# Q and K of the first two token tiles from padded weight rows on 32-column tiles of TensorE, with a reordered front of an adaLN, local-attention and MLP block

## The chip, the cores and the metric

The kernel runs on one core of a Trainium2 chip. The core has five engines that run side by side, each with its own queue of instructions: TensorE (PE; loads of its weights are listed as PEld), VectorE (DVE), ScalarE (ACT), GpSimd (POOL) and SyncE (SP), which here issues DMA transfers and DMA transposes. The metric is the device time of one execution in microseconds (us), and a kernel's time is the median of its runs.

## The reference, cut to what matters

One block over 2048 tokens of 448 features: an attention with a sliding dilated window (8 positions, 2 apart, 16 heads of 28 features), then an MLP with 1792 hidden features, both modulated by a condition c.

```python
mod = silu(c) @ w_mod                      # 448 -> 6 x 448
sa, ca, ga, sb, cb, gb = mod
h = layernorm(x) * (1 + ca) + sa
q, k, v = h @ wqkv                         # 16 heads of 28
attn = softmax(q . k[pos - 2*(0..7)] / sqrt(28))   # 8 keys for a token
x = x + ga * ((attn . v) @ wo)
h = layernorm(x) * (1 + cb) + sb
x = x + gb * (gelu(h @ w1 + b1) @ w2 + b2)
```

All inputs are bf16.

## The kernel before

**Tiles.** Tokens are held as eight tiles of 128 partitions; a partition holds two neighbouring tokens (even and odd), so the window of step 2 becomes 8 neighbouring columns of one parity. A contraction over 448 features is made of three steps of 128 rows and one of 64. The tail of 64 features is written twice into a tile, so that 64-row products can use either half of the rows.

**The front of a tile.** The rows of x are loaded (SP, L339, into x_all). DVE takes the statistics of each token (BN_STATS L456, BN_AGGR L458, into stt and mvs). The reciprocal deviation rs_all comes from ACT (Ln and Exp, L466 and L467) or POOL (a power, L469). DVE normalises into a buffer zy (L478), and the tail is copied (DVE L488 or L491, POOL L490). Tiles 0 and 1 are transposed by TensorE (L535, against ident, into PSUM ptr); tiles 2 to 7 by a DMA transpose (SP, L527, into zT). DVE (L502) or ACT (L504) then applies the modulation and writes hT, features by tokens.

**The modulation.** c is spread over partitions by TensorE into PSUM ps_c. silu(c) is made by ACT's exp (e_c, L392), DVE's add and reciprocal (L394, L395) and product (L396, silu_bf), and ACT widens it to 32 columns (L398, silu_bc). Products with w_mod give the columns of sa and ca (mod_col, L425, "column constants" below). The other four rows of the modulation come later from products on 32-column tiles of TensorE (L641).

**Q and K.** Attention needs Q and K with features on partitions, every head on 32 partitions. For tiles 0 and 1, `front_qk` takes the weights as the fixed side, four heads of 28 columns at a time. `spread` (L432 to L450) first copies the weight rows wqk_st and wqr_st into Wqk and Wqr, in which each head has 32 columns; these are ten copies on DVE, ACT and POOL. One product then covers four heads (128 columns) over 256 token columns: L562 in the first group, which goes row step by row step as the copies come, and L548 after it, with the 64-row step in L554. ACT (L609) copies each result to qT or kT. Tiles 2 to 7 (`natural_qk`) take hT as the fixed side and the weight rows as they are (L548 with wqk_st), and a DMA transpose puts the result into qT or kT. After tile 1 come the first scores (L738, PSUM lt) and the first value product (L706, PSUM pv).

**Order.** Nothing is scheduled at run time. Every step is recorded as a task with a number, its engine, what it reads and writes, and the buffers that it uses. `ORDER` lists the numbers in the sequence in which the tasks are written into the engines' queues; `n:A`, `n:D` or `n:P` puts a task on ACT, DVE or POOL, and `n+k@m` puts k dummy products on warm_w (L382) ahead of it, to fill TensorE's waits. `SLOTS` gives each buffer its place. Each queue runs in order. The loads go through SP in one sequence, and SP waits for an earlier transfer of the same one of eight lanes before it issues the next.

**Batches.** Attention runs in nine batches of 114 columns of each parity, with the tiles of the next batch prepared beside it; an output projection and the MLP of two tiles at a time follow as their batches are done.

## Time and profile before

| what | value |
|---|---|
| three runs | 168.0, 168.93, 170.48 us (median 168.93) |
| the profiled execution | 169.75 us, of which the span is 168.1 us |
| TensorE clock granted | 1.00 |
| TensorE busy | 161.5 us (96%) |
| DVE, ACT, POOL busy | 115.8 us (69%), 102.7 us (61%), 47.7 us (28%) |
| instructions | 4962 |
| DMA | 18.78 MB |

The span is what the profiler's instructions cover; 1.65 us of the profiled execution lie around it. Start times in the views count from the start of the span. A row of an engine's timeline gives the start in us, the length in us, the engine, the line, the operation with its result and operands, the tile or shapes, and how many instructions of that kind the row joins; in square brackets stands a wait ahead of it, with what ended it. Where a row joins several products of TensorE that run one behind the other, it ends a little later than the next row begins, since products overlap. In the view by stretches each engine is given by its busy time and, in brackets, the number of its instructions, in the order PE, PEld, DVE, ACT, POOL; then come the granted clock, the busy share of the DMA engines and GB/s. In the groups by line the columns are busy us and mean ns of one, then idle us ahead of it.

### The profile page before, as it was taken

The page shows a single profiled execution, that of the slowest core. Times are in us where ns is not written, and L with a number is a line of the kernel's source. Part 1 is how long each engine was busy: PE and PEld are TensorE (multiplying, and loading weights), DVE is VectorE, ACT ScalarE, POOL GpSimd, SP SyncE. Part 2 cuts the span into 40 slices and gives each one's busy share as a digit, 9 for nine tenths or more (in the row PEclk, how much of TensorE's full clock was granted, in tenths as well). Part 3 has the DMA queues.
Part 4 walks back from the last instruction along what each step waited for, and adds up shares of the span by engine and source line. Part 5 has one row for each costly group of instructions (what it writes and reads, how often), then busy time and mean ns, then how long its engine had stood idle before and what let it go on. Part 6 is the DMA issues. An engine that isn't in the chain of part 4 may idle for free.

```text
span 168.1 us, 4962 instructions
## 1 busy us (share of the span) xinstructions
PE 161.5 (96%) x2126; PEld 83.4 (50%) x2126; DVE 115.8 (69%) x271; ACT 102.7 (61%) x142; POOL 47.7 (28%) x76
## 2 busy tenths in 40 slices
PE   7989989999997999999999999999999999999992
PEld 4768544345544544435565444556434455444562
DVE  6869899879899689998738877474798930400032
ACT  3368987779489954759866376956627730097300
POOL 4135252300361201269300113820003870007200
PEclk9999999999999999999999999999999999999999
DMA  5999989799997999910091000008110027110003
GB/s 153 325 335 297 168 265 134 152 201 170 221 200 182 236 150 236 169 35 0 4 139 46 4 0 0 4 0 97 35 55 0 0 43 195 49 60 0 0 0 109
DMA packets 35574, 18.78 MB, mean 112 GB/s; under 512 B 28508, under 2 KB 34593, under 8 KB 35553
## 3 DMA queue, kind: packets, MB, share of 16 engines
q1 hardware_dynamic: 35548, 18.47, 53.0%
q8 instruction: 16, 0.26, 0.7%
q14 instruction: 6, 0.04, 0.1%
q10 hardware_dynamic: 4, 0.00, 0.0%
HBM read 9.81 MB, written 1.84 MB: 69 GB/s over the span
## 4 chain that ended last, share of the span: by engine, by line
PE 81%; DMA 10%; DVE 2%; POOL 2%; issue 1%; SPq 1%; ACT 1%; POOLq 0%; DVEq 0%
PE p L883 26%; PE p L548 22%; PE pw L803 7%; PE pq L548 6%; PE p L554 4%; DMA x_all<-in_A_x_dram 4%; PE po L771 3%; PE lt L738 3%; PE pv L706 3%; PE pv L548 3%; DMA wm_st<-in_w_mod_dram 3%; DMA zT<-zy 2%; DMA kT<-zy 2%; PE pq L554 1%; PE pd L760 1%
## 5 line engine op out<-in xcount | busy, mean ns | idle before, releaser
L864 ACT ACTIVATE hm<-p,b_col 128x512 bf16<-128x512 f32 x56 | 33.9, 692 | 29.9 <-PE p L554 27.3
L883 PE MATMUL p<-w_s,hm 128*128 128x448 bf16 (+1 forms) x238 | 44.1, 342 | 0.0
L548 PE MATMUL p<-yT,w_s 128*128 128x512 bf16 x168 | 38.1, 379 | 0.0
L469 POOL TENSOR_TENSOR rs_all<-mvs,neg_half 128x2 f32<-128x2 f32 x22 | 16.7, 766 | 57.9 <-DVE mvs L458 57.8
L883 PEld LDWEIGHTS <-hm 128*128 128x128 bf16 x238 | 22.7, 98 | 19.2 <-issue 0.8
L889 DVE TENSOR_TENSOR x_all<-p,x1p 128x896 bf16<-128x896 f32 (+2 forms) x10 | 8.9, 902 | 25.9 <-PE p L883 25.9
L548 PEld LDWEIGHTS <-w_s 128*128 128x128 bf16 x168 | 15.8, 98 | 20.9 <-issue 2.9
L456 DVE BATCH_NORM_STATS2 stt<-x_all 128x6 f32<-128x448 bf16 x32 | 18.7, 610 | 1.2 <-DMA x_all<-in_A_x_dram 1.0
L745 ACT ACTIVATE et<-lt 128x928 bf16<-128x928 f32 x18 | 16.1, 947 | 5.3 <-PE lt L738 5.1
L841 POOL TENSOR_TENSOR x1p<-x_all,gbb_bc 128x448 f32<-128x448 bf16 x16 | 17.8, 1134 | 0.0
L548 PE MATMUL pq<-wqk_st,hT 128*128 128x448 bf16 x72 | 15.2, 354 | 0.6 <-DVE hT L502 0.5
L788 DVE TENSOR_TENSOR qT<-po,den 128x912 bf16<-128x912 f32 x9 | 9.9, 1104 | 7.0 <-ACT den L782 5.6
L751 DVE TENSOR_TENSOR et<-et,mask 128x928 bf16<-128x928 bf16 x18 | 11.6, 672 | 2.4 <-ACT et L745 2.4
L803 PE MATMUL pw<-wo_s,qT 128*128 128x448 bf16 x64 | 13.2, 353 | 0.0
L780 ACT ACTIVATE den<-pd 128x928 f32<-128x928 f32 x9 | 8.5, 940 | 5.8 <-PE pd L760 5.7
L819 DVE TENSOR_TENSOR h<-h,mod_bc 128x896 bf16<-128x896 bf16 x16 | 11.1, 709 | 0.3
L548 PEld LDWEIGHTS <-hT 128*128 128x128 bf16 x72 | 6.4, 98 | 7.7 <-issue 1.3
L628 ACT CAST zy<-pq 128x896 bf16<-128x896 f32 x10 | 9.0, 906 | 2.0 <-PE pq L554 1.9
L810 DVE TENSOR_TENSOR x_all<-pw,x_all 128x896 bf16<-128x896 f32 x8 | 8.7, 1088 | 1.7 <-PE pw L803 1.5
L782 ACT ACTIVATE den<-den,den_bias 128x928 f32<-128x928 f32 x9 | 9.6, 1072 | 0.2
L478 DVE TENSOR_SCALAR zy<-h,mvs,rs_all 128x448 bf16<-128x448 bf16 x16 | 6.6, 456 | 4.4 <-POOL rs_all L469 4.3
L456 DVE BATCH_NORM_STATS2 stt<-h 128x6 f32<-128x448 bf16 x16 | 9.4, 613 | 0.2
(115 smaller groups left out, 183.4 us busy)
## 6 DMA issues: line engine op xcount, KB each, us to landing
w_s<-in_B_w_dram SPq DMA_DIRECT2D x7, 224.0 KB, 4.2
out_dram<-x_all SPq DMA_DIRECT2D x7, 224.0 KB, 2.2
x_all<-in_A_x_dram SPq DMA_DIRECT2D x3, 448.0 KB, 6.0
wmod<-in_w_mod_dram SPq DMA_DIRECT2D x3, 448.0 KB, 7.0
w_s<-in_B_w_dram SPq DMA_DIRECT2D x3, 448.0 KB
wqk_st<-in_A_wqkv_dram SPq DMA_DIRECT2D x3, 225.0 KB
wm_st<-in_w_mod_dram SPq DMA_DIRECT2D x1, 672.0 KB
x_all<-in_A_x_dram SPq DMA_DIRECT2D x2, 224.0 KB, 2.6
```

Source lines behind the costliest of these rows:

```text
L456: add("DVE", 0.53, lambda: nc.vector.bn_stats(out=stt[:, w, b, 0:6], in_=src()), reads=reads, bufs=bufs, after=early if w == b == 0 else ( ...
L469: ways = {"POOL": (0.55 + 0.17 * n, lambda: nc.gpsimd.tensor_tensor(out=r, in0=v, in1=neg_half[:, 0:n], op=ALU.pow))}
L548: nc.tensor.matmul(out(), lhsT=lhs(kt, slice(0, 128)), rhs=rhs(kt, slice(0, 128)), start=first and kt == 0, stop=not first and kt == KT - 2)
L745: exps.append(add("ACT", 0.83, lambda half=half, lt=lt: nc.scalar.activation(out=et.t[:, 2 * half:2 * half + 2].rearrange("p r m c -> p r ...
L751: nc.vector.tensor_tensor(out=ev, in0=ev, in1=mask[:], op=ALU.mult)
L782: exps.append(add("ACT", 0.96, lambda: nc.scalar.activation(out=den.t[:], in_=den.t[:], func=ACT.Exp, scale=-1.0, bias=den_bias[:]), bufs= ...
L788: nc.vector.tensor_tensor(out=qT[:, :, LEAD + q00:LEAD + q00 + 2 * WQ], in0=po.t[:, :, 0:NS * 4 * WQ].rearrange("p j (m c) -> p m j c", c=WQ),
L803: nc.tensor.matmul(pw.t[:, s, 0:D], lhsT=qT[:, KT * s + ft, LEAD + 128 * p:LEAD + 128 * p + 128], rhs=wo_s[:, ft, :], start=(ft == 0), sto ...
L819: add("DVE", 0.55, lambda vec=vec, op=op: nc.vector.tensor_tensor(out=h2.t[:], in0=h2.t[:], in1=vec.unsqueeze(1).to_broadcast([128, NS, D] ...
L841: add("POOL", 1.0, lambda n=n: nc.gpsimd.tensor_tensor(out=x1p.t[:, n, :], in0=xn(p, n), in1=gbb2_bc[:], op=ALU.add), reads=[f"x{p}", "gbb ...
L864: gelus.append(add("ACT", 0.585, lambda f=f, a=a, p1=p1s[g]: nc.scalar.activation(out=hm.t[:, f].rearrange("p n c -> p (n c)"), in_=p1.t[: ...
L883: nc.tensor.matmul(p2.t[:, n, 0:c1 - c0], lhsT=hm.t[:, f, n, q * 128:(q + 1) * 128], rhs=w2_s[:, f, c0:c1], start=(f == parts[0][0]), stop ...
```

## The change

1. **No spread copies.** `spread`, Wqk and Wqr are gone. `front_qk` reads the weight rows directly: one head with the 4 columns behind it makes a 32-column piece, and four pieces stand side by side on 32-column tiles of TensorE, each with the same 256 token columns. The rows that a head's piece has in excess (4 of 32) are those that nothing reads.
2. **Weight rows of 896 columns** are loaded instead of 900. The 4 columns behind the last head are set to zero by two memsets on DVE.
3. **One-step silu.** DVE's product writes silu_bc, 32 columns wide, at once; ACT's copy and silu_bf are gone.
4. **Tokens of tiles 2 and 3** come in two loads instead of one.
5. **Order.** The statistics of the first tile no longer stand behind all early memsets. `ORDER` and `SLOTS` are new throughout, since the numbers of the tasks have changed; fillers go from 35 to 28.

The core of the diff:

```diff
-    0, 0, 1, 1, 0, 0, 0, 0, 1, 2, 3, 0, 1, 0, 2, 3, ...          (SLOTS)
+    0, 0, 1, 1, 0, 0, 0, 2, 1, 3, 0, 0, 1, 2, 0, 3, ...
-3 14 17 0 1 15 5 9 10 18 11 16 13 19 20 2 6 24 21 73 55+12@55 26 ...   (ORDER)
+3 14 17 0 1 15 5 9 10 18 11 16 13 19 20 2 6 73 56+8@56 7 24 21 57 ...
-    wqk_st = sb("hm", [128, KT - 1, 2 * D + HP - DH], BF16, "wqk_st")
-    wqr_st = sb("h2", [128, 2 * D + HP - DH], BF16, "wqr_st")
+    wqk_st = sb("hm", [128, KT - 1, 2 * D + HP], BF16, "wqk_st")
+    wqr_st = sb("h2", [128, 2 * D + HP], BF16, "wqr_st")
...
+    def make_half():
+        nc.vector.memset(neg_half[:], -0.5)
+        nc.vector.memset(wqk_st.t[:, :, 2 * D:2 * D + HP - DH], 0.0)
+        nc.vector.memset(wqr_st.t[:, 2 * D:2 * D + HP - DH], 0.0)
...
-    load_x(2, 4)
+    load_x(2, 3)
+    load_x(3, 4)
...
-    add("DVE", 0.08, lambda: nc.vector.tensor_tensor(out=silu_bf[:], in0=e_c[:], in1=psc.t[:, 0, 0:128 * KT:128], op=ALU.mult),
-        reads=["e_c"], bufs=[psc], writes=["silu"], name="silu")
-    add("ACT", 0.18, lambda: nc.scalar.copy(out=silu_bc[:], in_=silu_bf[:].unsqueeze(2).to_broadcast([128, KT, HP])),
-        reads=["silu"], writes=["silu_bc"], name="silu_bc")
+    add("DVE", 0.2, lambda: nc.vector.tensor_tensor(
+        out=silu_bc[:], in0=e_c[:].unsqueeze(2).to_broadcast([128, KT, HP]),
+        in1=psc.t[:, 0, :].rearrange("p (k n) -> p k n", n=128)[:, :, 0:HP], op=ALU.mult),
+        reads=["e_c"], bufs=[psc], writes=["silu_bc"], name="silu_bc")
...
-        add("DVE", 0.53, lambda: nc.vector.bn_stats(...), after=early if w == b == 0 else (), ...
+        add("DVE", 0.53, lambda: nc.vector.bn_stats(...), ...
...
+                def piece(kts, i=i, half=half, pq=pq, state=state):
+                    for kt in kts:
+                        rest, first = kt == KT - 1, not state
+                        state.append(kt)
+                        for r, a in [(r, a) for r in range(4) for a in range(2)] if rest else [(r, a) for a in range(2) for r in range(4)]:
+                            rows = slice(KS * a, KS * a + KS) if rest else slice(0, 128)
+                            w = wqr_st.t[rows] if rest else wqk_st.t[:, kt]
+                            d0 = half * D + DH * (4 * (i + 2 * a) + r)
+                            nc.tensor.matmul(pq.t[HP * r:HP * r + HP, a, NS * 128 * i:NS * 128 * (i + 1)], lhsT=w[:, d0:d0 + HP],
+                                             rhs=hT[rows, NS * kt:NS * kt + NS, c0:c0 + 128], start=first, stop=len(state) == KT,
+                                             tile_position=(rows.start, HP * r))
...
-        if k == 0 and u[0] not in NATURAL:
-            spread(0)
-            spread(1)
```

Lines shift: BN_STATS is L438 after the change, BN_AGGR L440, rs_all on ACT L448 and L449, the norm L460, hT L484 (DVE) and L486 (ACT), the new products L566, the copy of Q and K L580.

The queues change as follows, at the places where the engines wait for one another. First DVE, from the first tile's BN_AGGR to the first copy for the modulation's products (zy_96 and zy_94 are the first tile's norm buffer). Before:

```order
L458 BN_AGGR mvs<-stt 128x2
L394 TENSOR_SCALAR e_c<-e_c 128x4 [waits Activation_49]
L395 RECIPROCAL e_c<-e_c 128x4 [waits DVE_49]
L478 TENSOR_SCALAR zy_96<-x_all,mvs,rs_all 128x448 [waits Activation_49,Pool_49]
L396 TENSOR_TENSOR silu_bf<-e_c,ps_c 128x4 [waits DVE_49,PE_49]
L418 COPY wm_d<-wm_st 128x6x64 [waits DMAHW3_49]
```

And now:

```order
L440 BN_AGGR mvs<-stt 128x2
L460 TENSOR_SCALAR zy_94<-x_all,mvs,rs_all 128x448 [waits DVE_49,Activation_49,Pool_49]
L396 TENSOR_SCALAR e_c<-e_c 128x4
L460 TENSOR_SCALAR zy_94<-x_all,mvs,rs_all 128x448 [waits DVE_49]
L397 RECIPROCAL e_c<-e_c 128x4 [waits DVE_49]
L398 TENSOR_TENSOR silu_bc<-e_c,ps_c 128x128 [waits DVE_49,PE_49]
```

The add and the reciprocal of silu stood ahead of the first norm and now stand behind it and behind the second.

Next DVE again, from the first tile's hT on; in both kernels the norms that follow are those of tile 1 (zy_96 before, zy_95 now). Before:

```order
L502 TENSOR_SCALAR hT<-ptr,mod_col 128x2x128
L439 COPY Wqk<-wqk_st 128x512 [waits DMAHW2_49]
L478 TENSOR_SCALAR zy_96<-x_all,mvs,rs_all 128x448 [waits Pool_49]
L478 TENSOR_SCALAR zy_96<-x_all,mvs,rs_all 128x448
L439 COPY Wqk<-wqk_st 128x512 [waits DMAHW3_49]
L491 COPY zy_96<-zy_96 128x2x64 [waits DVE_49]
L439 COPY Wqk<-wqk_st 128x512
L456 BN_STATS stt<-x_all 128x6 [waits DMAHW4_49]
```

And now:

```order
L460 TENSOR_SCALAR zy_95<-x_all,mvs,rs_all 128x448 [waits DVE_49,Activation_49,Pool_49]
L460 TENSOR_SCALAR zy_95<-x_all,mvs,rs_all 128x448
L438 BN_STATS stt<-x_all 128x6 [waits DMAHW4_49]
L438 BN_STATS stt<-x_all 128x6 [waits DMAHW5_49]
L438 BN_STATS stt<-x_all 128x6
L440 BN_AGGR mvs<-stt 128x2 [waits DVE_49]
L440 BN_AGGR mvs<-stt 128x2 x2
L438 BN_STATS stt<-x_all 128x6
L440 BN_AGGR mvs<-stt 128x2 [waits DVE_49]
L484 TENSOR_SCALAR hT<-ptr,mod_col 128x2x128 [waits PE_49]
```

The spread copies are gone, and a part of hT of tile 1 (L484, from ptr) now stands on DVE behind four statistics of tiles 2 and 3, of which the first two wait for the two loads. Before, ACT wrote all of tile 1's hT.

Last ACT, from the first tile's second hT copy to the first copy of Q. Before:

```order
L504 ACTIVATE hT<-ptr,mod_col 128x2x128
L449 COPY Wqr<-wqr_st 64x256
L504 ACTIVATE hT<-ptr,mod_col 128x2x128 [waits PE_49]
L504 ACTIVATE hT<-ptr,mod_col 128x2x128 x3
L609 CAST qT<-pq 128x8x128 [waits PE_49]
```

And now:

```order
L486 ACTIVATE hT<-ptr,mod_col 128x2x128
L486 ACTIVATE hT<-ptr,mod_col 128x2x128 [waits PE_49]
L486 ACTIVATE hT<-ptr,mod_col 128x2x128
L448 ACTIVATE rs_all<-mvs 128x2 [waits DVE_49]
L449 ACTIVATE rs_all<-rs_all 128x2 [waits Activation_49]
L486 ACTIVATE hT<-ptr,mod_col 128x2x128 [waits DVE_49]
L580 CAST qT<-pq 128x8x128 [waits PE_49]
```

ACT's last hT copy of tile 1 now stands behind a reciprocal deviation that waits for DVE's statistics of tile 2. On TensorE the new products of tile 0 and tile 1 stand in groups of 128-row and of 64-row pieces that alternate (wqk_st and wqr_st), with the transposes of tile 1 between them: from the first product of Q to the value product the shape of TensorE's tiles changes 15 times, against 6 before.

More of the change, by code (lines that the diff above doesn't have):

```diff
@@ L195 @@
     kT = cst.tile([128, 4 * NS, WT], BF16, name="kT")
-    Wqk = cst.tile([128, KT - 1, 2, H, HP], BF16, name="Wqk")
-    Wqr = cst.tile([128, 2, H // 2, HP], BF16, name="Wqr")
     Wv = cst.tile([128, KT, D], BF16, name="Wv")
@@ L222 @@
     e_c = cst.tile([128, KT], FP32, name="e_c")
-    silu_bf = cst.tile([128, KT], BF16, name="silu_bf")
     silu_bc = cst.tile([128, KT, HP], BF16, name="silu_bc")
@@ L244, with dconst @@
     early = []
-    def dconst(us, fn, writes):
-        early.append(add("DVE", us, fn, writes=writes, after=[one], name="const " + writes[0]))
+    def dconst(us, fn, writes, bufs=()):
+        early.append(add("DVE", us, fn, writes=writes, bufs=bufs, after=[one], name="const " + writes[0]))
     def const(us, fn, writes, reads=()):
@@ L430 @@
     modulation()
[L432 to L450 removed]
     exps, lt_mms, w1_mms, gelus = [], [], [], []
     def stats(src, w, b, reads, bufs=()):
[L456 removed]
+        add("DVE", 0.53, lambda: nc.vector.bn_stats(out=stt[:, w, b, 0:6], in_=src()), reads=reads, bufs=bufs,
             writes=[f"st{w}_{b}"], name="stats")
@@ L541, in front_ln, with summed @@
             affine(u, lambda kt: ptr[kt % 2].t[:, :, kt // 2], [(ptr[0], q) for q in range(np_)], ptr, True)
-    def summed(items, slot, reads, bufs, fills, name, after=(), split=None):
+    def summed(items, slot, reads, bufs, fills, name, after=()):
         def full(first):
@@ new lines, in front_qk @@
+            pq = psum("pq")
+            done = []
+            for i in range(2):
+                state = []
+                def piece(kts, i=i, half=half, pq=pq, state=state):
[9 more added lines that the diff above has]
+                                             tile_position=(rows.start, HP * r))
+                mine = []
+                for kts in [[kt] for kt in range(KT - 1)] if p == i == 0 else [list(range(KT - 1))]:
+                    mine.append(add("PE", 0.22 * len(kts), lambda kts=kts, piece=piece: piece(kts), reads=["wqpad"] + [f"wqk{kt}" for kt in kts] + [f"h{kt}_{p}" for kt in kts],
+                                    bufs=[pq, wqk_st], joins=[pq], after=done, mode="128x32", instr=16 * len(kts),
+                                    name=f"qk{p}_{half}{'ab'[i]}f" + (str(kts[0]) if len(kts) == 1 else "")))
+                mine.append(add("PE", 0.11, lambda piece=piece: piece([KT - 1]), reads=["wqpad", "wr0", "wr1", f"h{KT - 1}_{p}"],
+                                bufs=[pq, wqr_st], joins=[pq], after=done, mode="64x32", instr=16, name=f"qk{p}_{half}{'ab'[i]}r"))
+                done = mine
@@ L614, in natural_qk @@
+            dst = (kT if half else qT)[:, :, c0:c0 + 128].rearrange("p (s f) c -> p s f c", s=NS)
+            src = lambda pq=pq: pq.t[:].rearrange("p a (i s c) -> p s (a i) c", i=2, s=NS)
+            add("ACT", 0.91, lambda dst=dst, src=src: nc.scalar.copy(out=dst, in_=src()), bufs=[pq], writes=[f"{'qk'[half]}{ft}_{p}" for ft in range(4)],
+                alt={"DVE": (1.14, lambda dst=dst, src=src: nc.vector.tensor_copy(out=dst, in_=src()))}, name="evac_qk")
     def natural_qk(p):
```

105 lines of the change are left out of this document (25 added, 80 removed), and 24 rows, old and new, of tables (ORDER, SLOTS).

## The prediction

> **What bounds the kernel now.** The first part of the page gives the share of each engine, and the view by stretches the busy time of each engine in the first products of Q and K and from 33.71 on (us, busy us and instructions by engine, granted clock, DMA share, GB/s).
>
> ```profile
> PE 161.5 (96%) x2126; PEld 83.4 (50%) x2126; DVE 115.8 (69%) x271; ACT 102.7 (61%) x142; POOL 47.7 (28%) x76
> ...
> 9.26:12.04 2.78, 2.35 (x26) 1.74 (x24) 1.73 (x7) 1.68 (x5) 1.03 (x2) 1.00 0.97 335
> ...
> 33.71:163.20 129.49, 128.62 (x1650) 63.21 (x1651) 86.30 (x169) 79.57 (x107) 35.56 (x43) 1.00 0.45 82
> ```
>
> From 33.71 us to the end TensorE is busy for 128.62 of 129.49 us at full clock. Names and sequence of its tasks are the same there in both kernels, so whatever the change does must show as the time at which TensorE gets there. The view of the chain that ended last tells what sets that time.
>
> ```profile
> 6.32 6.00 DMA x_all<-in_A_x_dram
> ...
> 17.56 3.38 DMA zT<-zy
> ...
> 21.04 1.71 DVE hT L502 x3
> ```
>
> At the front it is not TensorE that is late, but the tokens of tiles 2 and 3: their load lands at 12.32, their transposes at 20.94, and DVE has copied their hT at 22.75. TensorE's own timeline shows how long it would have taken without that (start, us, operation, count).
>
> ```profile
> 9.26 0.38 PE L562 MATMUL pq<-hT,Wqk 128*128 128x256 bf16 x2
> 9.47 0.49 PE L382 MATMUL pq<-warm_w 128*128 128x256 bf16 x3
> ...
> 11.05 0.39 PE L562 MATMUL pq<-hT,Wqk 128*128 128x256 bf16 x2 [0.43 <-DVE Wqk L439]
> 11.28 0.61 PE L535 MATMUL ptr<-ident,zy 128*128 128x128 bf16 x8
> ...
> 12.04 0.61 PE L554 MATMUL pq<-hT,Wqr 64*128 64x256 bf16 x8
> 12.58 2.79 PE L548 MATMUL pq<-hT,Wqk 128*128 128x256 bf16 x24
> 15.31 0.61 PE L554 MATMUL pq<-hT,Wqr 64*128 64x256 bf16 x8
> 15.85 0.44 PE L738 MATMUL lt<-qT,kT 28*64 28x58 bf16 x32
> ...
> 17.64 1.64 PE L706 MATMUL pv<-Wv,hT 128*64 128x448 bf16 x16
> ...
> 21.89 0.36 PE L548 MATMUL pq<-wqk_st,hT 128*128 128x448 bf16 x1
> 22.79 2.25 PE L548 MATMUL pq<-wqk_st,hT 128*128 128x448 bf16 x11 [0.54 <-DVE hT L502]
> ...
> 29.18 2.44 PE L548 MATMUL pq<-wqk_st,hT 128*128 128x448 bf16 x12
> ...
> 33.71 0.70 PE L738 MATMUL lt<-qT,kT 28*64 28x58 bf16 x64 [0.36 <-DMA kT<-zy]
> ```
>
> Twelve such products take 2.44 us undisturbed (29.18); from 21.89 they would have ended at 24.33, and ended at 25.04. **TensorE has 0.71 us in hand here**, and 0.36 us more ahead of 33.71, where it waits for the transposed K. Up to 1.07 us lost on tiles 0 and 1 is given back; nothing won there alone counts.
>
> **The change, part by part.** *Products of Q and K, tiles 0 and 1.* One 128-column product becomes four on 32-column tiles. The kernel has this form already in the modulation rows (L641):
>
> ```profile
> 27.03 1.05 PE L641 MATMUL pb<-wmod,silu_bc 128*32 128x448 bf16 x16
> ...
> 27.03 0.31 PEld L641 LDWEIGHTS <-silu_bc 128*32 128x32 bf16 x12 [0.36 <-issue]
> ...
> L641 PEld LDWEIGHTS <-silu_bc 128*32 128x32 bf16 x12 | 0.2, 95 | 0.4 <-issue 0.4
> ...
> L548 PE MATMUL pq<-hT,Wqk 128*128 128x256 bf16 x36 | 4.3, 273 | 0.0
> ```
>
> A product's row holds 0.17 us in which the next already runs: 24 of 256 columns end in 2.79 us, and with 0.273 for one that makes (2.79 - 0.273) / 23 = 0.109 each. In the same way a full one of 448 columns takes (2.44 - 0.36) / 11 = 0.19, and sixteen in a row would take 3.0 us. They end in 1.05: four rounds of four side by side, with twelve loads done in the first 0.31 us, under running products. Hence four tiles cost what one full product costs, 0.109 us at 256 columns. Both kernels then hold 48 such rounds, and 16 half-row products at 0.055 (8 in 0.61 - 0.17 = 0.44), 6.1 us for both tiles. **Difference nothing; bounds** 0 and one round of loads in the open for each of 48 rounds, 48 x 0.095 = 4.6 us. I take 0, since the row at 27.03 is of that very form; its stream is longer (448 columns, not 256), which is why the other end stays.
>
> [...]
>
> *Changes of tile shape.* Between two shapes TensorE stands: 12.58 + 2.62 = 15.20, next start 15.31, so 0.11; at 12.04 + 0.44 = 12.48, next 12.58, 0.10. From the first Q product to the value product (17.64) the old order has 6 such changes, the new one 15, since pieces of 128 and 64 rows alternate and the transposes stand between them: **+9 x 0.11 = +1.0 us**. Bounds 0 (shapes of equal columns might not drain) and 1.0.
>
> *The ten spread copies go.* They cost TensorE the filler at 9.47 and the wait at 11.05: 9.26 to 17.64 is 8.38 us, and 6.1 + 0.45 (transposes, 0.61 less 0.17) + 0.27 (scores) + 6 x 0.11 is 7.48. **0.9 us goes**, if nothing else is late. The copies also leave DVE (three), ACT (four) and POOL (three); those had time.
>
> *What is late next: DVE.* Its timeline:
>
> ```profile
> 3.42 0.63 DVE L456 BATCH_NORM_STATS2 stt<-x_all 128x6 f32<-128x448 bf16 x1
> ...
> 4.18 0.63 DVE L456 BATCH_NORM_STATS2 stt<-x_all 128x6 f32<-128x448 bf16 x1
> ...
> 5.02 0.13 DVE L394 TENSOR_SCALAR e_c<-e_c 128x4 f32<-128x4 f32 x1
> 5.18 0.18 DVE L395 RECIPROCAL e_c<-e_c 128x4 f32<-128x4 f32 x1
> 5.69 0.40 DVE L478 TENSOR_SCALAR zy<-x_all,mvs,rs_all 128x448 bf16<-128x448 bf16 x1 [0.33 <-ACT rs_all L467]
> 6.00 0.15 DVE L396 TENSOR_TENSOR silu_bf<-e_c,ps_c 128x4 bf16<-128x4 f32 x1
> ...
> 8.07 0.15 DVE L425 TENSOR_TENSOR mod_col<-ps_col,add_col 128x8 f32<-128x8 f32 x1
> ...
> 8.60 0.73 DVE L502 TENSOR_SCALAR hT<-ptr,mod_col 128x256 bf16<-128x256 bf16 x2
> ...
> 12.34 1.68 DVE L456 BATCH_NORM_STATS2 stt<-x_all 128x6 f32<-128x448 bf16 x3 [1.05 <-DMA x_all<-in_A_x_dram]
> 13.94 0.31 DVE L458 BATCH_NORM_AGGREGATE mvs<-stt 128x2 f32<-128x9 f32 x2
> ```
>
> ACT's hT copies, rstd and Q and K copies, SP's transposes and POOL's tail of tile 2:
>
> ```profile
> 5.14 0.20 ACT L466 ACTIVATE rs_all<-mvs 128x2 f32<-128x2 f32 x1 [0.39 <-DVE e_c L394]
> ...
> 8.59 0.56 ACT L504 ACTIVATE hT<-ptr,mod_col 128x256 bf16<-128x256 bf16 x1 [0.39 <-DVE mod_col L425]
> ...
> 11.93 1.93 ACT L504 ACTIVATE hT<-ptr,mod_col 128x256 bf16<-128x256 bf16 x4 [1.10 <-PE ptr L535]
> 13.74 1.02 ACT L609 CAST qT<-pq 128x1024 bf16<-128x1024 f32 x1
> 14.63 1.04 ACT L609 CAST kT<-pq 128x1024 bf16<-128x1024 f32 x1
> ...
> 16.12 2.74 SPq L527 DMA_TRANSPOSE zT<-zy  x2
> ...
> 17.17 0.29 POOL L490 COPY zy<-zy 128x128 bf16<-128x128 bf16 x1
> ```
>
> From the first norm (5.69) to the column constants (8.07) DVE is never idle, so its queue, not the modulation products, sets 8.07. The add and the reciprocal (0.13 + 0.18) filled its wait ahead of 5.69 and now stand behind it; the silu step, now 128 wide, lies between 0.15 (as 4 wide) and 0.37 (one of the 256-wide reads of PSUM at 8.60): I take 0.28, +0.13. ACT's copy of it (0.30) goes but was not what ended last. The memsets between the first two statistics leave their place (start to start 0.76 against 0.53 in the group at 12.34, -0.2) and stand behind them; they and the two new pad memsets cost 0 to 0.2 there, I take 0.1. Sum **+0.3**: constants at 8.4, ACT's first hT (0.52 behind the constants, 0.56 long) at 9.5, first product at 9.6.
>
> Now the walk. To the end of tile 1's transposes there are 12 rounds (1.31), 3 half-row pieces (0.33), 6 changes (0.66) and the transposes (0.45): 9.6 + 2.75 is 12.35, against 11.73 with 10 rounds done. Then 12 rounds (1.31), a half-row piece and three changes (0.44): 14.1. The next needs hT of tile 1 from DVE, which now stands behind **four statistics of tiles 2 and 3**, the second of them on the load of tile 3. Their load was 448 KB, landing at 12.32. Apart, tile 3 lands at about the same time and tile 2 some 0.9 us sooner (224 KB at the 260 KB/us that the queue gave up to 12.32); the 896-column rows save at most 0.3. So: 12.1 + 3 x 0.53 + four aggregates (0.5, two in 0.31) + 0.4 for the copy is 14.6. **TensorE waits 0.5** (bounds 0 and 0.9, by a landing 0.5 sooner or 0.4 later). ACT likewise takes two rstd (two steps, 0.44 together) between its hT copies, so its q and k copies (0.89 start to start, and 1.04) run from 15.15 to 17.1, and the scores that need them start at 17.2. TensorE, after 12 rounds, four half-row pieces and four changes (2.2 us), would be there at 16.8: **+0.4**. Scores, 12 rounds and two changes (0.27 + 1.31 + 0.22) put the value product at **19.0 against 17.64: +1.36** (bounds -0.5, with neither added changes nor waits, and +1.8).
>
> *The other engines and queues.* POOL builds mask1 at once and no longer ahead of tile 2's tail (17.17), so SP issues the second of its two transposes not at 17.5 but, 1.37 behind the first, at 16.9 to 17.3; they land at 20.3 to 20.7, and the three hT copies (1.71) end by 22.5. On SP the same bytes go in one more instruction (0.5 us of issue, behind which other loads stand; the queue was full anyway). wqk1 passes the two remainder loads, whose products come after its own now.
>
> **Sum.** From the value product to 21.89 nothing changes (4.25 us): TensorE comes to tile 2 at 23.25, finds hT ready, and ends the twelve products at 25.69 instead of 25.04: 1.36 - 0.71 = +0.65. Of it 0.36 goes into the wait at 33.71, which hangs on SP's queue and not on TensorE. **+0.3 us on the span of 168.1**, 170.05 for an execution like the profiled one (169.75, of which 1.65 lie around the span). That execution lies 0.8 above the median of the three runs; on the median the forecast is 168.93 + 0.3 = **169.2**.
>
> **Rivals.**
> 1. *Loads in the open (slower).* If a round of 256 columns is too short to hide four loads of 32 columns, each of the 48 rounds pays 0.095: +4.6, all behind the slack that is already used, 169.2 + 4.6 = 173.8. It decides once the round takes more than 0.109. Against it: twelve loads in 0.31 us. For it: 0.31 / 3 = 0.10 for four loads is hardly less than the round.
> 2. *Tile 1 later still, no token earlier.* Where tile 2's part lands no sooner and tile 3's late, DVE's copy comes at 15.2, and ACT's behind it: +0.5 to +0.8 more, 169.9. For it: the loads share one queue, at a DMA share of 0.97 (9.26 to 12.04).
> 3. *TensorE keeps its lead (the change does what it is named for).* If shape changes cost nothing and tile 1's waits are covered, the value product comes by 18.1, tile 2's hT at 22.3 sets the time, and SP's chain comes forward by the same 0.4: 168.5. Against it: each change in the trace costs 0.10 to 0.11.
>
> **How the numbers follow.** Forecast 0.50 (168.6 to 169.9), rival 2 0.17, rival 3 0.20, rival 1 0.08; 0.05 for what I do not see, TensorE's instruction fetch for one: its queue holds 370 rows more. Faster or slower by 2% (3.4 us, about what a measurement of this kernel can tell from no change) needs rival 1, or something unseen: faster 0.03, within 0.87, slower 0.10. The range starts at rival 3 and ends at rival 2; the three runs (168.0 to 170.48) spread by more than either step, so it is 167.9 to 171.0.
>
> **What would show it.** Rounds of four starting 0.107 to 0.11 apart, some 0.11 between shapes; constants near 8.4; a wait of TensorE for hT near 14.2 to 14.8; the value product near 19; no wait at tile 2, and none for the transposed K near 33.7. A value product before 18.1 makes rival 3 right, rounds of 0.2 us rival 1.

## The result: 3% slower, and the profile after

| | kernel before | changed kernel |
|---|---|---|
| median of 4 runs | 168.49 us (168.0 to 170.48) | 174.28 us (174.25 to 174.43) |
| ratio | 1 | 1.031, interval 1.026 to 1.036 |
| span of the profiled execution | 168.1 us | 172.5 us |
| TensorE products in the trace | 2126 | 2311 |

The forecast was 169.2, within 167.9 to 171.0. Ratios, here and below, leave out runs that lie over 1.5% above the fastest of the same kernel, among them the profiled executions of again, before_dense and dense_shift; medians and ranges are those of all runs.

The page of the changed kernel, its first part, the instruction queue among the DMA queues (packets, MB, share) and the chain that ended last:

```profile
PE 162.5 (94%) x2311; PEld 83.4 (48%) x2311; DVE 114.9 (67%) x269; ACT 100.6 (58%) x140; POOL 45.5 (26%) x73
...
q8 instruction: 18, 0.29, 0.7%
...
PE 90%; issue 3%; DMA 3%; DVE 1%; SPq 1%; DVEq 0%
```

TensorE does about the same busy time (162.5 against 161.5) in a span 4.4 us longer. (The medians lie 5.8 apart: the profiled execution of the kernel before, 169.75 us, is one of its longer ones, so that the views explain the 4.5 us up to 174.25.) What has grown is "issue" in the chain: 3% where the kernel before has 1%, time in which the engine waits for nothing that the profile names. TensorE's timeline says where:

```profile
10.18 0.84 PE L566 MATMUL pq<-hT,wqk_st 128*32 128x256 bf16 x24
10.95 0.30 PE L566 MATMUL pq<-hT,wqr_st 64*32 64x256 bf16 x8
...
13.09 1.50 PE L566 MATMUL pq<-hT,wqk_st 128*32 128x256 bf16 x48
...
14.74 0.62 PE L566 MATMUL pq<-hT,wqk_st 128*32 128x256 bf16 x15
16.25 0.50 PE L566 MATMUL pq<-hT,wqk_st 128*32 128x256 bf16 x9 [0.90 <-issue]
...
18.51 1.05 PE L566 MATMUL pq<-hT,wqk_st 128*32 128x256 bf16 x31
22.18 0.72 PE L566 MATMUL pq<-hT,wqk_st 128*32 128x256 bf16 x17 [2.61 <-issue]
22.83 1.64 PE L676 MATMUL pv<-Wv,hT 128*64 128x448 bf16 x16
...
27.28 0.34 PE L708 MATMUL lt<-qT,kT 28*64 28x58 bf16 x17 [0.37 <-issue]
27.55 2.44 PE L530 MATMUL pq<-wqk_st,hT 128*128 128x448 bf16 x12
...
38.02 0.70 PE L708 MATMUL lt<-qT,kT 28*64 28x58 bf16 x64
...
44.34 0.20 PE L741 MATMUL po<-et,vb 64*32 64x57 bf16 x2 [0.93 <-issue]
```

The new products themselves run as fast as forecast: 48 of them, twelve rounds, in 1.50 us. But TensorE stands twice in the middle of a group, after 15 products of 24 and after 31 of 48, where no new operand begins. Together that is 3.51 us ahead of the value product, which comes at 22.83 instead of 17.64 (+5.19). The rest of the +5.19 is the first product (10.18 instead of 9.26, +0.92) and 0.76 between it and the value product. By 38.02, the row that stood at 33.71, +4.31 is left. Behind it a stretch of 0.93 is new at 44.34, and one of 0.85 that the kernel before has at 51.90 is gone; the span ends 4.4 us later.

In the whole sequence of products, the restarts at 16.25, 22.18 and 27.28 are exactly 128 products apart, 256 instructions with their weight loads. The page lists q8 as an instruction queue; its packets in the trace are of 16,384 bytes, 18 of them here and 16 before. Counted in steps of 128 products from a restart (16.25 here, 51.90 in the kernel before), there are 18 blocks of 256 instructions here from the one entered at 10.96 on, and 16 before from the one entered at 11.83 on, the last of each short: as many as packets. Below, a packet is therefore read as bringing the block behind the one that TensorE is in; the profile itself does not say what a packet holds. The view of the DMA queues over two short stretches of the changed kernel catches the two packets that lie ahead of the two restarts. From 13.7 to 15.0:

```profile
q1 hardware_dynamic: 276, 0.48, 100.7%
q8 instruction: 1, 0.02, 5.1%
```

and from 18.2 to 21.0:

```profile
q1 hardware_dynamic: 621, 0.19, 113.5%
q8 instruction: 1, 0.02, 5.7%
```

In the list of packets the first runs from 13.82 to 14.89 and the second from 18.27 to 20.82; TensorE restarts 1.36 us behind the end of each. The table gives the same for all kernels whose front is compared below: when TensorE begins a block of 256 instructions, how long after that the next packet starts, when it ends, and how long TensorE then stands at the next block's first instruction. The entry is read at the block's fourth product, 0.01 to 0.34 us behind its first (16.27 and 16.25 in the changed kernel).

| kernel | first block entered | packet starts behind it | packet ends | stretch | second entered | packet starts behind it | packet ends | stretch | value product |
|---|---|---|---|---|---|---|---|---|---|
| before | 11.83 | 3.16 | 16.11 | none | 19.43 | 0.83 | 21.55 | none | 17.64 |
| changed | 10.96 | 2.86 | 14.89 | 0.90 | 16.27 | 2.00 | 20.82 | 2.61 | 22.83 |
| changed, again | 12.02 | 3.16 | 16.25 | 1.39 | 17.82 | 2.36 | 21.29 | 1.51 | 23.29 |
| wide | 12.25 | 2.61 | 15.98 | none | 20.44 | 2.79 | 24.22 | none | 18.28 |
| half | 10.50 | 3.34 | 14.87 | 0.19 | 16.61 | 1.62 | 19.28 | none | 18.61 |
| shift | 10.36 | 1.77 | 13.23 | none | 15.12 | 1.33 | 17.71 | 0.54 | 20.40 |
| shift_timed | 9.49 | 3.05 | 13.56 | 0.97 | 14.96 | 1.34 | 17.24 | 0.29 | 20.09 |
| quiet | 10.41 | 4.05 | 15.58 | 1.99 | 16.82 | 1.90 | 19.66 | none | 21.86 |
| cols | 9.92 | 2.23 | 13.13 | none | 15.47 | 0.36 | 16.91 | none | 19.24 |
| thin | 10.55 | 1.27 | 12.93 | none | 14.79 | 0.73 | 16.46 | none | 18.46 |
| spread_back | 13.76 | 2.23 | 17.32 | none | 21.49 | 2.70 | 25.14 | none | 19.34 |
| before_dense | 10.41 | 2.91 | 14.50 | 1.71 (ACT) | 16.04 | 3.07 | 20.15 | 2.40 | 22.17 |
| dense_shift | 8.79 | 2.67 | 12.42 | 0.22 | 13.71 | 3.07 | 18.02 | 2.53 | 21.89 |
| dense_thin | 11.69 | 0.13 | 12.78 | none | 15.43 | 0.30 | 17.02 | none | 19.07 |

### The profile page after: what moved, and what is told of

It reads as the page before. It is cut to its first block, busy times and chain, and to the rows that moved or that the text cites. A ratio compares the mean times of both kernels' runs of the same rounds, so it can differ in the third digit from the quotient of the medians.

```text
span 172.5 us, 5325 instructions
## 1 busy us (share of the span) xinstructions
PE 162.5 (94%) x2311; PEld 83.4 (48%) x2311; DVE 114.9 (67%) x269; ACT 100.6 (58%) x140; POOL 45.5 (26%) x73
## 4 chain that ended last, share of the span: by engine, by line
PE 90%; issue 3%; DMA 3%; DVE 1%; SPq 1%; DVEq 0%
PE p L853 25%; PE p L530 22%; PE pq L530 8%; PE pw L773 7%; PE pq L566 5%; PE pv L676 5%; PE p L536 4%; PE lt L708 4%; PE po L741 3%; DMA wm_r<-in_w_mod_dram 3%; PE pv L530 3%; PE pq L536 2%; PE pd L730 1%; DVE stt L438 1%; PE pq L384 1%
## 5 line engine op out<-in xcount | busy, mean ns | idle before, releaser
L451 POOL TENSOR_TENSOR rs_all<-mvs,neg_half 128x2 f32<-128x2 f32 x20 | 15.1, 759 | 60.8 <-DVE mvs L440 60.8
L438 DVE BATCH_NORM_STATS2 stt<-x_all 128x6 f32<-128x448 bf16 x32 | 18.7, 609 | 2.2 <-DMA x_all<-in_A_x_dram 2.0
L811 POOL TENSOR_TENSOR x1p<-x_all,gbb_bc 128x448 f32<-128x448 bf16 x16 | 18.2, 1159 | 0.3 <-POOL seen L838 0.3
L721 DVE TENSOR_TENSOR et<-et,mask 128x928 bf16<-128x928 bf16 x18 | 10.9, 634 | 5.1 <-ACT et L715 5.1
L566 PE MATMUL pq<-hT,wqk_st 128*32 128x256 bf16 x192 | 7.1, 275 | 3.5 <-issue 3.5
L460 DVE TENSOR_SCALAR zy<-h,mvs,rs_all 128x448 bf16<-128x448 bf16 x16 | 6.6, 456 | 4.7 <-POOL rs_all L451 4.7
L438 DVE BATCH_NORM_STATS2 stt<-h 128x6 f32<-128x448 bf16 x16 | 9.4, 612 | 0.2
```

The costliest lines, as they stand in the source:

```text
L438: add("DVE", 0.53, lambda: nc.vector.bn_stats(out=stt[:, w, b, 0:6], in_=src()), reads=reads, bufs=bufs, writes=[f"st{w}_{b}"], name="stats")
L451: ways = {"POOL": (0.55 + 0.17 * n, lambda: nc.gpsimd.tensor_tensor(out=r, in0=v, in1=neg_half[:, 0:n], op=ALU.pow))}
L566: nc.tensor.matmul(pq.t[HP * r:HP * r + HP, a, NS * 128 * i:NS * 128 * (i + 1)], lhsT=w[:, d0:d0 + HP], rhs=hT[rows, NS * kt:NS * kt + NS, ...
L721: nc.vector.tensor_tensor(out=ev, in0=ev, in1=mask[:], op=ALU.mult)
L811: add("POOL", 1.0, lambda n=n: nc.gpsimd.tensor_tensor(out=x1p.t[:, n, :], in0=xn(p, n), in1=gbb2_bc[:], op=ALU.add), reads=[f"x{p}", "gbb ...
```

## The experiments

**Theory A**: TensorE runs out of instructions. Its program arrives in blocks of 256; the packet with the next block starts 0.13 to 4.05 us after TensorE enters the one before it (table), and where a block is used up faster than the next one comes, TensorE stands. **Theory B**: the stretches are waits for data. **Theory C**: the weights of the four pieces load in the open. **Theory D**: order and loads of the change made the time, and the products only share it. The expectations count the blocks of the changed kernel from another zero: 11.43 and 14.29 there are 10.96 and 13.82 in the views.

### wide: a quarter of the instructions in the new products

```diff
-                        for r, a in [(r, a) for r in range(4) for a in range(2)] if rest else [(r, a) for a in range(2) for r in range(4)]:
-                            nc.tensor.matmul(pq.t[HP * r:HP * r + HP, a, ...], lhsT=w[:, d0:d0 + HP], ...
+                        for a in range(2):
+                            d0 = min(half * D + DH * 4 * (i + 2 * a), 2 * D - 128)
+                            nc.tensor.matmul(pq.t[:, a, ...], lhsT=w[:, d0:d0 + 128], ...
```

> The changed kernel, but each group of four 32-column products is one 128-column product over 128 neighbouring weight columns, without the pads between heads (so Q and K of tiles 0 and 1 hold other values): 4240 instructions on TensorE instead of 4624, the rest of the order untouched. Theory A (TensorE runs out of instructions: its program arrives in blocks of 256, and the two idle stretches of 0.90 and 2.61 us marked issue are late blocks): both stretches go, the value product comes at 19.3 instead of 22.83 (22.83 - 3.51), TensorE then waits for hT of tile 2 at 24.8 at the latest, and the time is 169.6 to 171.6. Theory B (the stretches are waits for data or for buffers that the view fails to name): they stay, 173.8 to 174.6. Theory C (the weights of four pieces load in the open): rounds of four become shorter than the 0.109 us in which they start now, and the stretches stay.

Measured: 169.48 us (168.29 to 170.66), 1.0047 of the kernel before, interval 1.0003 to 1.0091. TensorE's timeline:

```profile
16.49 0.44 PE L708 MATMUL lt<-qT,kT 28*64 28x58 bf16 x32 [0.34 <-ACT kT L580]
...
18.28 1.64 PE L676 MATMUL pv<-Wv,hT 128*64 128x448 bf16 x16
```

Both stretches are gone, the value product comes 4.55 us sooner, and 4.8 of the 5.8 us go with them. A holds, and a little more came back than it expected: 0.65 of the 4.55 is the first product, which comes at 9.53 instead of 10.18. B, which left 173.8 or more, falls. C falls on the rounds: 0.111 us each in the changed kernel (1.50 less 0.28, over 11), against 0.109 in the kernel before.

### shift and shift_timed: the same work, 56 instructions later in the program

```diff
-            nc.tensor.matmul(t.sums[0].t[:, 0, 0:256], lhsT=warm_w[:, 0:128], rhs=warm_w[:, 0:256], start=True, stop=True)
+            for c in (0, 128):
+                nc.tensor.matmul(t.sums[0].t[:, 0, c:c + 128], lhsT=warm_w[:, 0:128], rhs=warm_w[:, c:c + 128], start=True, stop=True)
```

> The changed kernel with each of the 28 dummy products split into two of half the columns: 28 more products, 56 more instructions, all ahead of the first product of Q, in about the same time. Theory A: the stretches stay at the same instruction of TensorE's program, so they come 28 products earlier among the 256 new ones: ahead of number 115 instead of 143, and of number 211 instead of 239; the time is within 1% of 174.3. Theory B: they stay ahead of the same products, 143 and 239.

The one run took 170.75 us, 2% less than expected, with one stretch (0.54, ahead of product 211, counted from 0) and none at 143, 239 or 115. It was run again, nine times:

> The changed kernel with each dummy product in two halves (56 more instructions ahead of Q), now timed. If the shift itself took the second stretch away, the block boundary now standing where its fetch meets fewer transposes: 170.3 to 171.3, clear of the changed kernel in the same comparison. If its single run was chance: the same time as the changed kernel in this comparison, within 0.6%.

Measured: 170.32 us (169.72 to 174.43), 1.0064 of the kernel before, interval 1.0034 to 1.0094. Its timeline:

```profile
12.60 1.38 PE L567 MATMUL pq<-hT,wqk_st 128*32 128x256 bf16 x43
14.95 0.39 PE L567 MATMUL pq<-hT,wqk_st 128*32 128x256 bf16 x5 [0.97 <-issue]
...
18.68 1.48 PE L567 MATMUL pq<-hT,wqk_st 128*32 128x256 bf16 x45 [0.29 <-issue]
20.09 1.64 PE L677 MATMUL pv<-Wv,hT 128*64 128x448 bf16 x16
```

With the products of the rows between, the two stretches stand ahead of products 115 and 211, 28 earlier each, as A says: the place is a place in the program, not one in the data. This settles A against B. That the sum falls from 3.51 to 1.26 was not expected: the block in which the products begin is entered at 9.49 here, during the dummy products, and the packet with the next starts 2.84 us behind the first product of Q instead of 3.64.

### quiet and thin: fewer loads beside the packets

In quiet the seven loads of w_mod and wo move in ORDER behind the two transposes of tiles 2 and 3 (35, 37, 41, 34, 39, 36, 40 behind 131).

> The changed kernel with the loads of the modulation's weights and of wo, seven in all, issued only behind the two transposes of tile 2 and 3, so that little but tokens and Wv moves from 13 to 18 us; the later modulation products come late by that, so only the front is compared. Theory A with a part for the traffic: the first block is fetched at 12.3 to 13.5 instead of 14.29, and the first stretch is 0.4 us or less instead of 0.90; the second stays between 1.0 and 2.6, since the transposes still run beside its fetch. Theory A without traffic: 0.90 and 2.61 stay within 0.2. Theory B says nothing of either.

```profile
16.81 0.56 PE L543 MATMUL pq<-hT,wqk_st 128*32 128x256 bf16 x9 [1.99 <-issue]
```

The first stretch grew to 1.99, and its packet started 4.05 us behind the block instead of 2.86: a miss. The second, expected between 1.0 and 2.6, is gone, but that proves little: the granted clock was about 0.5 there (0.56 and 0.50 in the rows of the last section), and the block lasted 4.4 us instead of 3.3, so its follower had more time. The one run took 174.46 us. The tokens of tiles 4 to 7 were still in the queues (DMA share 0.93 from 13 to 14 us). So thin moves those too:

```diff
 ORDER: SP    ... 27 28 -33 29 31 -32 -35 30 -37 140 131 +32 +33 +35 +37 41 34 ...
 ORDER: DVE, POOL   190 188 189 259 261 260 197 199 191 198 200 201 192 behind 142 (tile 2's hT)
```

> The changed kernel with the loads of the tokens of tiles 4 to 7 and of the modulation's weights moved behind the transposes of tiles 2 and 3, and the statistics of tiles 4 to 7 behind tile 2's hT, so that the queue has little left from 11 to 17 us; only the front up to the value product is compared, since later work is late by the move. If the loads make the blocks late: the first block is fetched within 1.2 us of TensorE's entering the one before it (11.43 there; 2.86 us in the changed kernel) and so is the second (2.00), no stretch of more than 0.4 us stands before the value product, which comes at 19.0 to 19.9. If the loads have no part in it: the two fetches start 2 to 3 us behind, and the stretches of about 0.9 and 2.6 us stay.

The view by stretches of thin (PE, PEld, DVE, ACT, POOL busy; clock; DMA share; GB/s):

```profile
12.00:13.00 1.00, 1.00 (x28) 0.77 (x24) 0.97 (x5) 0.33 (x1) 0.00 (x0) 1.00 0.00 0
13.00:14.00 1.00, 1.00 (x44) 0.88 (x36) 0.96 (x5) 0.81 (x3) 0.70 (x1) 1.00 0.00 0
14.00:15.00 1.00, 1.00 (x40) 0.66 (x32) 1.00 (x5) 0.97 (x4) 0.19 (x1) 1.00 0.00 0
```

and of the changed kernel:

```profile
12.00:13.00 1.00, 1.00 (x32) 0.65 (x24) 0.88 (x3) 0.00 (x0) 0.01 (x1) 1.00 0.93 269
13.00:14.00 1.00, 1.00 (x39) 0.90 (x40) 0.96 (x5) 0.92 (x2) 0.23 (x1) 1.00 1.04 332
14.00:15.00 1.00, 1.00 (x44) 0.66 (x35) 0.96 (x5) 0.55 (x4) 0.47 (x1) 1.00 1.02 379
```

With the queues empty from 12 to 15 us (DMA share 0.00 against about 1) the packets start 1.27 and 0.73 us behind the block, no stretch is left, and TensorE goes from its first product to the value product in 8.69 us:

```profile
9.77 0.84 PE L543 MATMUL pq<-hT,wqk_st 128*32 128x256 bf16 x24
...
18.46 1.64 PE L653 MATMUL pv<-Wv,hT 128*64 128x448 bf16 x16
```

The first packet came 0.07 later than the 1.2 expected; the value product even earlier than expected. The full execution takes 175.85 us, since the loads that were put off are late for later work (TensorE waits 2.29 us for wmod ahead of 29.73 and 0.93 ahead of 31.23); it is no remedy.

### cols: the other order on DVE ahead of the column constants

In ORDER, 62 and 61 (copies of the large weight rows) go ahead of 67, 66 behind it, and 98, 100, 99, 12 (tile 1's statistics, a constant) behind 83.

> The changed kernel with another order on DVE ahead of the column constants: the copies of the large weight rows stand ahead of the two of the remainder, and the statistics of tile 1 behind the column constants. The constants come at 8.5 to 8.7 instead of 9.44 and the first product of Q at 9.3 to 9.5 instead of 10.18. If the front sets the time up to tile 2 (no block of instructions late by its own clock), all of it arrives: 173.3 to 173.6. If the late blocks set it (theory A, with the second fetch held by the transposes on SP and not by TensorE's pace), the second stretch grows by what the first products gain, and the time is 173.8 to 174.4.

Measured: 172.63 us (171.17 to 172.76), 1.0148 of the kernel before, interval 1.0063 to 1.0233.

```profile
9.14 0.84 PE L543 MATMUL pq<-hT,wqk_st 128*32 128x256 bf16 x24
...
11.67 0.40 PE L543 MATMUL pq<-hT,wqk_st 128*32 128x256 bf16 x8 [1.13 <-ACT hT L463]
...
19.24 1.64 PE L653 MATMUL pv<-Wv,hT 128*64 128x448 bf16 x16
```

The first product comes 1.04 us sooner. A wait of 1.13 for ACT, whose hT copy now stands behind a late reciprocal deviation, takes that back, but it lies inside the dense products and gives the first packet time (the block lasts 5.55 us; in the changed kernel its work is 4.4); the second starts only 0.36 us behind its block. No stretch is left ahead of the value product. Neither expected time was met; both left out that the wait of 1.13 for data could take the place of the 0.90 for instructions. The value product comes 3.59 us sooner than in the changed kernel, and yet the execution is only 1.62 us shorter (172.63 against 174.25), since a block's edge costs more further on:

```profile
40.84 0.20 PE L718 MATMUL po<-et,vb 64*32 64x57 bf16 x2 [1.42 <-issue]
```

There the packet ended at 39.46, 1.38 ahead of the restart; in the changed kernel the same edge cost 0.93 (44.34). From 41 to 44 us the granted clock is 0.50, where the changed kernel has 1.00 behind its stretch.

### spread_back, before_silu_x: what the rest of the change costs

spread_back puts Wqk, Wqr, the ten copies and the 128-column products back into the changed kernel; before_silu_x makes silu in one step in the kernel before, and issues two loads for tiles 2 and 3.

> The changed kernel with the ten spread copies and the 128-column products of the kernel before put back, and all else of the change kept (one-step silu, tokens of tiles 2 and 3 apart, its order): 4240 instructions on TensorE. Theory A: no stretch marked issue before the value product, which comes at 18.3 to 19.3; 169.0 to 170.6, the kernel with wide products (169.48) and at most 1 us for the copies; what is then left to the kernel before is the order's price. Theory D (the order and the loads made the time, the products only share it): 172 or more.

> The kernel before with the two small edits alone: silu in one step on DVE, and the tokens of tiles 2 and 3 in two loads issued one behind the other. By the sums: +0.13 on DVE's queue ahead of the column constants, and tile 2's statistics sooner by at most 0.9: TensorE's wait of 0.54 for tile 2 shrinks by 0 to 0.5. 168.0 to 168.9 beside a kernel before of 168.5, no difference. If the two edits carry part of the loss (theory D): 169.5 or more.

Measured: spread_back 169.51 us (169.07 to 171.96), 1.0051, interval 1.0007 to 1.0096; before_silu_x 168.85 us (168.02 to 170.93), 1.0001, interval 0.9955 to 1.0048. In spread_back no stretch stands ahead of the value product, which comes 0.04 later than expected:

```profile
19.34 1.64 PE L654 MATMUL pv<-Wv,hT 128*64 128x448 bf16 x16
```

So D falls once more. Silu and the two loads make no difference that can be measured; what the change costs without its 32-column pieces is 0.5%, some 0.9 us. By what is left it would be the order's, but no run has the order alone.

### before_dense, dense_thin, dense_shift: the pieces alone, in the kernel before

```diff
+        def four(out, lhs, rhs, kt, rows, start, stop):
+            for r in range(4):
+                nc.tensor.matmul(out()[HP * r:HP * r + HP], lhsT=lhs(kt, rows, r), rhs=rhs(kt, rows), start=start, stop=stop,
+                                 tile_position=(rows.start, HP * r))
```

takes the place of each product in `front_qk` of the kernel before; `spread` copies nothing. Order, loads and silu are the old ones.

> The kernel before with one part of the change alone: Q and K of tiles 0 and 1 as four 32-column products each, read straight from the weight rows, without the spread copies; old order, old loads, old silu: 4638 instructions on TensorE instead of 4254. If the pieces cost nothing but shape changes (the prediction's forecast): no stretch marked issue before the value product, 168.0 to 169.3. Theory A: one or two such stretches, 128 products apart, 1.5 to 4 us together, less the 1.07 that this kernel has in hand: 169.4 to 172.

Measured: 172.6 us (170.33 to 173.57), 1.011, interval 1.0015 to 1.0204. The four runs took 170.33, 171.79, 173.4 and 173.57 us, and the profile is of the last, so the stretches below are those of a long execution; their sum (4.11) and the median lie a little above A's range. Its timelines of products and of weight loads:

```profile
16.03 1.28 PE L556 MATMUL pq<-hT,wqk_st 128*32 128x256 bf16 x40 [1.71 <-ACT kT L624]
...
21.40 0.84 PE L556 MATMUL pq<-hT,wqk_st 128*32 128x256 bf16 x24 [2.40 <-issue]
22.17 1.64 PE L721 MATMUL pv<-Wv,hT 128*64 128x448 bf16 x16
```

```profile
16.03 0.99 PEld L556 LDWEIGHTS <-wqk_st 128*32 128x32 bf16 x39 [1.89 <-issue]
```

The part that carries the change's name makes the long stretch by itself, 128 products behind the first. By the ratios, though, it costs 1.1% alone and the rest of the change 0.5%, less together than the 2.4 to 3.1% of the whole; what the difference comes from is not shown. The first can be read in two ways: the products' row names ACT, which makes a PSUM buffer free at this very instruction, and the weight loads' row names "issue". ACT's row

```profile
14.53 1.04 ACT L624 CAST kT<-pq 128x1024 bf16<-128x1024 f32 x1
```

ends at 15.57, 0.46 ahead of the restart, and the packet at 14.50, 1.53 ahead of it. The stretch begins at 14.32. The wait for ACT alone would thus have cost 1.25, and the block alone at least 1.4, if TensorE restarts 1.23 us or more behind a packet's end as at the other edges of the table (1.23 in quiet, 1.25 to 1.57 at the rest). The two lie side by side, and beyond ACT's wait the block adds 0.46 at most.

The same move of loads as in thin, and the same split of dummy products as in shift, in this kernel:

> The kernel before with the 32-column pieces alone, and the loads of the tokens of tiles 4 to 7 and of the modulation's weights moved behind the transposes of tiles 2 and 3 (the statistics of tiles 4 to 7 behind tile 2's hT); only the front is compared, later work is late by the move. If full queues make the blocks late: the two fetches start within 1.5 us of TensorE's entering the block before (2.91 and 3.07 with the loads there), the stretches ahead of the value product sum to 0.8 us or less (1.70 and 2.40 there), and it comes at 17.6 to 18.9 instead of 22.17. If the same move in the changed kernel helped by chance: the fetches start 2 to 3 us behind and the stretches sum to 2 us or more.

```profile
13.00:14.00 1.00, 1.00 (x46) 0.58 (x48) 1.00 (x3) 0.90 (x2) 0.00 (x0) 1.00 0.00 1
14.00:15.00 1.00, 1.00 (x44) 0.98 (x41) 1.00 (x6) 1.00 (x4) 0.61 (x1) 1.00 0.00 0
```

```profile
19.07 1.64 PE L697 MATMUL pv<-Wv,hT 128*64 128x448 bf16 x16
```

The packets start 0.13 and 0.30 us behind the block and no stretch is left; the value product misses its range by 0.17, since the first products came later (10.68 instead of 9.41). That the packets start sooner once the loads are moved away is now seen in two kernels, in one execution of each: 2.86 and 2.00 us behind the block became 1.27 and 0.73, 2.91 and 3.07 became 0.13 and 0.30. The full execution here took 176.79 us, again with the put-off loads late.

> The kernel before with the 32-column pieces alone, and each of its 35 dummy products split into two halves: 70 more instructions, most of them ahead of the first product. The first edge of a block (196 in the sequence, in the first products without the split) then lies in the dummy products, so the block behind it is asked for earlier. If what counts is how the dense stretch lies on the blocks: the stretches ahead of the value product sum to 0.3 to 2.0 instead of 4.10, and the time is 169.0 to 171.0. If the gain of the shift in the changed kernel had another cause: 171.5 to 173.5, as without the split.

Measured: 172.26 us (170.53 to 173.42), 1.0121, interval 1.0027 to 1.0215: no gain, a miss. The time lies in the range of the other branch, by which the gain in the changed kernel had another cause.

```profile
13.70 2.25 PE L557 MATMUL pq<-hT,wqk_st 128*32 128x256 bf16 x75 [0.22 <-issue]
...
19.35 0.28 PE L754 MATMUL lt<-qT,kT 28*64 28x58 bf16 x11 [2.53 <-issue]
```

The first stretch shrank to 0.22, but the second packet again started 3.07 us behind its block. Where TensorE stands in the runs of the table, it stands at such an edge, wherever the split puts it, and goes on 1.23 to 1.57 us behind the end of the packet. Why the second packet came sooner in shift_timed (1.34 behind its block) than in the changed kernel (2.00) or here is thus open.

### half, before_shift, again

half is the changed kernel with wide products in tile 1 only; before_shift is the kernel before with its 35 dummy products split in two.

> The changed kernel with tile 1's products as in the run with wide products (128 neighbouring columns, so Q and K of tile 1 hold other values), and tile 0's as they are: 4432 instructions on TensorE. Theory A: the first stretch stays where it is (the block's edge lies 15 products into tile 1), 0 to 1.2 us; the second goes, since the next 256 instructions now last over 6 us; the value product at 18.5 to 20.0, 169.3 to 171.0. If late blocks are not about the number of instructions: as the changed kernel.

Measured: 170.07 us (169.04 to 171.79), 1.0038, interval 0.9997 to 1.0080; 0.19 is left of the first stretch, nothing of the second, the value product comes at 18.61. A's ranges held for the stretches, the value product and the time; the next 256 instructions last 5.96 us, not quite the 6 that it named.

> The kernel before with each of its 35 dummy products split into two of half the columns: 70 more instructions ahead of the first product of Q. Its profile has one stretch marked issue, 0.85 us at 51.90, ahead of product 302 of the scores' line. Theory A: that one is a late block too, so it stands 35 products earlier, ahead of number 267 of that line (or is gone, if that block comes in time), and none stands at 302; the time is within 1% of the kernel before. Theory B: it stays at 302.

Measured: 169.67 us (168.32 to 172.05), 1.0064, interval 1.0014 to 1.0114. The kernel before has

```profile
51.90 0.34 PE L738 MATMUL lt<-qT,kT 28*64 28x58 bf16 x18 [0.85 <-issue]
```

and the same 64 products of before_shift run in one piece:

```profile
50.12 0.75 PE L739 MATMUL lt<-qT,kT 28*64 28x58 bf16 x64
```

As A allows, none stands at 302; none stands at 267 either, where the edge should now be, since that block's packet ended at 44.97, 5 us ahead of it. One more run speaks for the place: before_silu_x has the same products on TensorE in the same sequence, and stands at the same one of them for a shorter time:

```profile
50.92 0.34 PE L743 MATMUL lt<-qT,kT 28*64 28x58 bf16 x18 [0.22 <-issue]
```

The time did not follow the 0.85 us; the executions of before_shift spread over 3.7 us.

> The changed kernel once more, in more runs and beside the others. Theory A, where a block's lateness depends on how fast the loads move in that run: the median lies between 171 and 174.5 with a spread of 1 us or more, as the four runs at 174.3 were alike but a shift by 56 instructions gave 170.75 in one run. If the position of the blocks alone sets it: 174.2 to 174.5 in every run.

Measured: 174.81 us (172.78 to 175.87), 1.0243 of the kernel before, interval 1.0163 to 1.0323, with stretches of 1.39 and 1.51. The places are the same, the lengths are not: a spread of 3.1 us where the first four runs had 0.2. That speaks for A and against equal runs; the median lies 0.31 above A's range.

## Why the prediction was wrong, point by point

- **The front decides, the rest follows.** Right. +5.19 at the value product became +4.31 behind the scores at 38.02; 0.88 was given back where 1.07 was forecast, with a new stretch of 0.37 (27.28) in between; the waits for tile 2 (row at 27.55) and for the transposed K (38.02) are gone, as forecast.
- **Four pieces cost what one product costs.** Right: 0.111 us a round, where 0.109 was forecast and rival 1 needed about 0.2. Rival 1, loads in the open, gave nearly the measured time (173.8) for a cause that is not there. A time that fits is no proof of its cause.
- **Changes of shape, 0.11 each.** Right: six rounds from 10.18 end at 10.85, the next group starts at 10.95. In thin, with nothing to wait for, 8.69 us lie between first product and value product, against a sum of work of 6.1 + 0.45 + 0.27 + 15 x 0.11 = 8.47.
- **Waits for tile 1's hT and its Q and K, 0.5 and 0.4.** Not seen. In thin they are missing; in the changed kernel they would lie under the first stretch.
- **Column constants +0.3.** Mis-sized: they end at 9.44 instead of 8.50, +0.94. DVE's timeline, first the last of them before, then the changed kernel:

```profile
8.33 0.17 DVE L425 TENSOR_TENSOR mod_col<-ps_col,mod_col 128x8 f32<-128x8 f32 x1
```

```profile
7.21 0.18 DVE L420 COPY wm_d<-wm_r 128x64 bf16<-128x64 bf16 x1 [0.43 <-DMA wm_r<-in_w_mod_dram]
...
7.53 0.43 DVE L420 COPY wm_d<-wm_st 128x384 bf16<-128x384 bf16 x2
7.87 0.62 DVE L438 BATCH_NORM_STATS2 stt<-x_all 128x6 f32<-128x448 bf16 x1
8.41 0.16 DVE L420 COPY wm_d<-wm_r 128x64 bf16<-128x64 bf16 x1
...
9.27 0.17 DVE L427 TENSOR_TENSOR mod_col<-ps_col,mod_col 128x8 f32<-128x8 f32 x1
```

  The sum took the operations that moved and not the queue they moved into: the first copy now stands ahead of the large ones and waits 0.43 for a load, and a statistic of 0.62 stands ahead of the last copy. cols, which undoes that, starts its products at 9.14.
- **The step that failed** stands among the chances, "0.05 for what I do not see, TensorE's instruction fetch for one: its queue holds 370 rows more". The 370 rows got a chance and no price, and the bounds of the new products had no term for them: waiting for instructions was put at nothing, and it took 3.51 us ahead of the value product. The price could have been worked out from the kernel before: at this stage the packet with the next block starts 3.16 us behind the entry into a block and takes 1.12, and at 51.90, where TensorE does wait for one, it restarts 1.24 behind the packet's end. That is an estimate of 5.5 us for a block under full queues. A block of nothing but 128-column products would last 128 x 0.109 = 14 us (the one entered at 11.83, with scores and half-row products in it, lasts 7.6); a block of 32-column pieces lasts 32 rounds, 3.5 us. Two edges lie in the new products: 2 x (5.5 - 3.5) = 4.0, where 3.51 was measured. The blocks' own work is 4.4 and 3.3 us, which gives 1.1 and 2.2 for stretches of 0.90 and 2.61. That it comes so near is in part luck: with loads in the queues the packets of the table start anywhere from 0.36 to 4.05 us behind their blocks. The stretch of 0.85 at 51.90 was in the profile, in the densest work that the kernel had, and went unexplained.

What stays open: what makes a packet start 0.36 us behind its block in cols and 4.05 in quiet, with loads in the queues both times. That it is shorter with empty queues is shown (1.27, 0.73, 0.13 and 0.30 us in thin and dense_thin); which transfer holds it up in a given run is not. No version here beat the kernel before.

## What to carry to other kernels

Count the instructions per microsecond as well as the work: splitting one product into four on column tiles kept TensorE's time here (0.111 us a round against 0.109 for one product) and used up its program four times as fast. Where 256 instructions last less than about 5.5 us (the estimate above) while loads fill the queues, look for a stop at the block's edge: in the table TensorE stood at 12 of 15 such edges (a block's time taken without the stretch), but not in shift behind a block of 4.8 us, in quiet behind one of 4.4, nor in cols behind one of 3.2, whose followers came in time. In a profile, look for "issue" in the middle of a group of equal products and for restarts a fixed number of instructions apart (256 here); the proof is to shift the program by some instructions and see whether the place moves with it.
